# x + alpha * fx on one core: chunks of 16 rows with a tail of smaller ones, and alpha spread by a matmul

One core of one Trainium2 chip. The metric is the time of the kernel on the device in microseconds (us); lower is better. "Span" is the time from the first to the last instruction in the profile; the measured time is some 1.8 us longer. "Fast" means that a run agrees with the fastest of its kernel.

## The reference

```python
B, S, D = 512, 32, 640          # bf16
def reference(x, fx, alpha):    # alpha: one number
    return x + alpha * fx
```

The arrays are 16384 rows of 640 numbers. Each of the 128 partitions takes 128 consecutive rows, a row being 1280 bytes. 41.94 MB are read and 20.97 MB written.

## The kernel before

```python
    alpha_bf = const_pool.tile([P, 1], alpha.dtype, name="alpha_bf")
    nc.sync.dma_start(out=alpha_bf[:], in_=alpha.to_broadcast((P, 1)))
    alpha_t = const_pool.tile([P, 1], mybir.dt.float32, name="alpha_t")
    nc.vector.tensor_copy(out=alpha_t[:], in_=alpha_bf[:])

    for c in range(nchunks):                       # 16 chunks, CH = 8 rows, io_pool has bufs=4
        rs = slice(c * CH, (c + 1) * CH)
        xt = io_pool.tile([P, CH, D], x.dtype, name="xt")
        ft = io_pool.tile([P, CH, D], fx.dtype, name="ft")
        nc.sync.dma_start(out=xt[:], in_=xv[:, rs, :])
        nc.sync.dma_start(out=ft[:], in_=fxv[:, rs, :])
        nc.vector.scalar_tensor_tensor(out=xt[:], in0=ft[:], scalar=alpha_t[:, 0:1], in1=xt[:],
                                       op0=..., op1=...)   # cut: mult, then add
        nc.scalar.dma_start(out=ov[:, rs, :], in_=xt[:])
```

Loads go out on the SP queue, stores on the ACT queue. In every transfer a partition's share of a chunk is one contiguous run; I call it a *piece* (10,240 bytes here). A transfer is 128 pieces, and the packet records show 16 completion records for it (2048 pieces and 256 such records for the 16 stores), which I read as 8 pieces of each transfer on each of the 16 DMA engines.

Of the kernel before, what the change touches and what calls it, by code (L numbers as in the profile page):

```python
# [1 line left out]

# [4 lines left out]


@with_exitstack  # L10
def kernel(
    ctx: ExitStack,
    tc: tile.TileContext,
    x: bass.AP,
    fx: bass.AP,
    alpha: bass.AP,
    out: bass.AP,
):
    nc = tc.nc
    P = nc.NUM_PARTITIONS  # L20

    xf = x.flatten_outer_dims()
    fxf = fx.flatten_outer_dims()
    of = out.flatten_outer_dims()
    N, D = xf.shape
    assert N % P == 0, (N, P)
    rows_per_part = N // P

    xv = xf.rearrange("(p n) d -> p n d", p=P)
    fxv = fxf.rearrange("(p n) d -> p n d", p=P)  # L30
    ov = of.rearrange("(p n) d -> p n d", p=P)

    CH = 1
    for cand in (8, 4, 2, 1):
        if rows_per_part % cand == 0:
            CH = cand
            break
    nchunks = rows_per_part // CH

    const_pool = ctx.enter_context(tc.tile_pool(name="const", bufs=1))  # L40
    io_pool = ctx.enter_context(tc.tile_pool(name="io", bufs=4))

    alpha_bf = const_pool.tile([P, 1], alpha.dtype, name="alpha_bf")
    nc.sync.dma_start(out=alpha_bf[:], in_=alpha.to_broadcast((P, 1)))  # L44
    alpha_t = const_pool.tile([P, 1], mybir.dt.float32, name="alpha_t")
    nc.vector.tensor_copy(out=alpha_t[:], in_=alpha_bf[:])  # L46

    for c in range(nchunks):
        rs = slice(c * CH, (c + 1) * CH)
        xt = io_pool.tile([P, CH, D], x.dtype, name="xt")  # L50
        ft = io_pool.tile([P, CH, D], fx.dtype, name="ft")
        nc.sync.dma_start(out=xt[:], in_=xv[:, rs, :])  # L52
        nc.sync.dma_start(out=ft[:], in_=fxv[:, rs, :])
        nc.vector.scalar_tensor_tensor(  # L54
            out=xt[:],
            in0=ft[:],
            scalar=alpha_t[:, 0:1],
            in1=xt[:],
            op0=mybir.AluOpType.mult,
            op1=mybir.AluOpType.add,  # L60
        )
        nc.scalar.dma_start(out=ov[:, rs, :], in_=xt[:])


# [1 line left out]
_INS = ['x', 'fx', 'alpha']  # L66
_OUTS = [((512, 32, 640), 'bfloat16')]


# [23 lines left out]
```

## Time and profile before

| | before |
|---|---|
| time, median of 4 runs | 158.67 us (158.57 to 158.87) |
| span of the profiled run | 156.8 us |
| VectorE busy | 89.0 us, 57% |
| bytes moved | 62.92 MB, 401 GB/s over the span |
| no transfer at all near the end | 148.5 to 152.4 us |

The engines that move data are the bound: they are full from about 4 us to 148 (DMA share 1.01 from 4 to 16 and from 20 to 146 us). VectorE has time to spare, except behind the very last load, where nothing is left to run beside it. The prediction shows the lines.

### The profile page before, as it was taken

The page shows a single profiled execution, that of the slowest core. Times are in us where ns is not written, and L with a number is a line of the kernel's source. Part 1 is how long each engine was busy: PE and PEld are TensorE (multiplying, and loading weights), DVE is VectorE, ACT ScalarE, POOL GpSimd, SP SyncE. Part 2 cuts the span into 40 slices and gives each one's busy share as a digit, 9 for nine tenths or more (in the row PEclk, how much of TensorE's full clock was granted, in tenths as well). Part 3 has the DMA queues.
Part 4 walks back from the last instruction along what each step waited for, and adds up shares of the span by engine and source line. Part 5 has one row for each costly group of instructions (what it writes and reads, how often), then busy time and mean ns, then how long its engine had stood idle before and what let it go on. Part 6 is the DMA issues. An engine that isn't in the chain of part 4 may idle for free.

```text
span 156.8 us, 154 instructions
## 1 busy us (share of the span) xinstructions
DVE 89.0 (57%) x17; POOL 0.2 (0%) x4
## 2 busy tenths in 40 slices
DVE  0029873908558292855919285491927649193760
POOL 0000000000000000000000000000000000000000
DMA  3999999999999999999999999999999999999716
GB/s 60 410 428 426 392 400 421 428 434 434 421 428 434 431 426 423 436 428 426 431 431 426 426 434 431 423 426 426 439 423 426 426 436 426 426 423 436 316 76 259
DMA packets 7056, 62.92 MB, mean 401 GB/s; under 512 B 912, under 2 KB 912, under 8 KB 912
## 3 DMA queue, kind: packets, MB, share of 16 engines
q1 hardware_dynamic: 4752, 41.95, 64.1%
q10 hardware_dynamic: 2304, 20.97, 31.6%
HBM read 41.94 MB, written 20.97 MB: 401 GB/s over the span
## 4 chain that ended last, share of the span: by engine, by line
DMA 80%; DVE 14%; SPq 1%; issue 1%; DVEq 0%
DMA ft<-in_fx_dram 61%; DMA out_dram<-xt 19%; DVE xt L54 14%; SPq L52 1%; SPq L44 0%; DVEq L54 0%
## 5 line engine op out<-in xcount | busy, mean ns | idle before, releaser
L54 DVE SCALAR_TENSOR_TENSOR xt<-ft,alpha_t,xt 128x5120 bf16<-128x5120 bf16 x16 | 88.8, 5552 | 58.7 <-DMA ft<-in_fx_dram 58.7
L46 DVE CAST alpha_t<-alpha_bf 128x1 f32<-128x1 bf16 x1 | 0.2, 154 | 3.8 <-DMA alpha_bf<-in_alpha_dram 3.8
L77 POOL MEMSET const-bfloat16-1.0<- 128x1 bf16 x1 | 0.1, 101 | 0.0
L77 POOL MEMSET const-uint8-127<- 128x1 uint8 x1 | 0.1, 101 | 0.0
L77 POOL MEMSET const-float32-0.0<- 128x1 f32 x1 | 0.1, 98 | 0.2 <-issue 0.2
L77 POOL MEMSET const-float32-1.0<- 128x1 f32 x1 | 0.1, 98 | 0.0
## 6 DMA issues: line engine op xcount, KB each, us to landing
xt<-in_x_dram SPq DMA_DIRECT2D x16, 1280.0 KB, 17.3
ft<-in_fx_dram SPq DMA_DIRECT2D x16, 1280.0 KB, 20.4
out_dram<-xt ACTq DMA_DIRECT2D x16, 1280.0 KB, 10.2
alpha_bf<-in_alpha_dram SPq DMA_DIRECT2D x1, 0.2 KB, 3.1
```

The lines of the kernel that those rows point to most:

```text
L46: nc.vector.tensor_copy(out=alpha_t[:], in_=alpha_bf[:])
L52: nc.sync.dma_start(out=xt[:], in_=xv[:, rs, :])
L54: nc.vector.scalar_tensor_tensor(out=xt[:], in0=ft[:], scalar=alpha_t[:, 0:1], in1=xt[:], op0=mybir.AluOpType.mult, op1=mybir.AluOpType.add,)
L77: nc = _bacc.Bacc("TRN2", target_bir_lowering=False, num_devices=1)
```

## The change

It means to cut fixed costs: fewer and larger transfers in the middle (16 rows, three buffers), a tail of 8, 4 and 4 rows with buffers of their own so that less is exposed at the end, and alpha read as one element and spread to the partitions by a matmul with a row of ones, off the queue of the loads.

```diff
-    io_pool = ctx.enter_context(tc.tile_pool(name="io", bufs=4))
-    alpha_bf = const_pool.tile([P, 1], alpha.dtype, name="alpha_bf")
-    nc.sync.dma_start(out=alpha_bf[:], in_=alpha.to_broadcast((P, 1)))
+    alpha_sb = const_pool.tile([1, 1], alpha.dtype, name="alpha_sb")
+    nc.scalar.dma_start(out=alpha_sb[:], in_=alpha.rearrange("(a b) -> a b", b=1))
+    ones_row = const_pool.tile([1, P], alpha.dtype, name="ones_row")
+    nc.vector.memset(ones_row[:], 1.0)
+    alpha_ps = psum_pool.tile([P, 1], mybir.dt.float32, name="alpha_ps")
+    nc.tensor.matmul(alpha_ps[:], ones_row[:], alpha_sb[:], start=True, stop=True)
     alpha_t = const_pool.tile([P, 1], mybir.dt.float32, name="alpha_t")
-    nc.vector.tensor_copy(out=alpha_t[:], in_=alpha_bf[:])
+    nc.vector.tensor_copy(out=alpha_t[:], in_=alpha_ps[:])
 ... (cut: a function that would choose the sizes; it is overridden by the next line)
+        sizes = [16] * 7 + [8, 4, 4]
+        x_pool = ctx.enter_context(tc.tile_pool(name="xio", bufs=MAIN_BUFS))     # 3
+        f_pool = ctx.enter_context(tc.tile_pool(name="fio", bufs=MAIN_BUFS))     # 3
+        tail_pool = ctx.enter_context(tc.tile_pool(name="tail", bufs=1))
+        for ci, ch in enumerate(sizes):
+            if ch == MAX_CH:                                                     # 16
+                xt = x_pool.tile([P, MAX_CH, D], x.dtype, name="xt")
+                ft = f_pool.tile([P, MAX_CH, D], fx.dtype, name="ft")
+            else:
+                xt = tail_pool.tile([P, ch, D], x.dtype, name="xt", tag=f"xt_t{ci}")
+                ft = tail_pool.tile([P, ch, D], fx.dtype, name="ft", tag=f"ft_t{ci}")
 ... (cut: loads, compute and store as before)
```

More of the change, by code (lines that the diff above doesn't have):

```diff
@@ L7, with _chunk_schedule @@
 from concourse._compat import with_exitstack
+def _chunk_schedule(rows_per_part: int, max_ch: int) -> list[int]:
+    tail = []
+    c = max_ch // 2
+    t = 0
+    while c >= 1:
+        tail.append(c)
+        t += c
+        if c == 1:
+            tail.append(1)
+            t += 1
+            break
+        c //= 2
+    sizes = []
+    remaining = rows_per_part
+    while remaining - max_ch >= t:
+        sizes.append(max_ch)
+        remaining -= max_ch
+    while remaining > t:
+        c = min(max_ch, remaining - t)
+        sizes.append(c)
+        remaining -= c
+    for c in tail:
+        if remaining <= 0:
+            break
+        c = min(c, remaining)
+        sizes.append(c)
+        remaining -= c
+    if remaining > 0:
+        sizes.append(remaining)
+    assert sum(sizes) == rows_per_part, (sizes, rows_per_part)
+    assert all(s >= 1 for s in sizes), sizes
+    return sizes
 @with_exitstack
@@ L20 @@
     P = nc.NUM_PARTITIONS
+    dsize = mybir.dt.size(x.dtype)
     xf = x.flatten_outer_dims()
@@ L25 @@
     N, D = xf.shape
-    assert N % P == 0, (N, P)
-    rows_per_part = N // P
-    xv = xf.rearrange("(p n) d -> p n d", p=P)
-    fxv = fxf.rearrange("(p n) d -> p n d", p=P)
-    ov = of.rearrange("(p n) d -> p n d", p=P)
-    CH = 1
-    for cand in (8, 4, 2, 1):
-        if rows_per_part % cand == 0:
-            CH = cand
-            break
-    nchunks = rows_per_part // CH
-    const_pool = ctx.enter_context(tc.tile_pool(name="const", bufs=1))
-    io_pool = ctx.enter_context(tc.tile_pool(name="io", bufs=4))
@@ L43 @@
-    alpha_bf = const_pool.tile([P, 1], alpha.dtype, name="alpha_bf")
-    nc.sync.dma_start(out=alpha_bf[:], in_=alpha.to_broadcast((P, 1)))
-    alpha_t = const_pool.tile([P, 1], mybir.dt.float32, name="alpha_t")
-    nc.vector.tensor_copy(out=alpha_t[:], in_=alpha_bf[:])
-    for c in range(nchunks):
-        rs = slice(c * CH, (c + 1) * CH)
-        xt = io_pool.tile([P, CH, D], x.dtype, name="xt")
-        ft = io_pool.tile([P, CH, D], fx.dtype, name="ft")
-        nc.sync.dma_start(out=xt[:], in_=xv[:, rs, :])
-        nc.sync.dma_start(out=ft[:], in_=fxv[:, rs, :])
-        nc.vector.scalar_tensor_tensor(
-            out=xt[:],
-            in0=ft[:],
-            scalar=alpha_t[:, 0:1],
-            in1=xt[:],
-            op0=mybir.AluOpType.mult,
-            op1=mybir.AluOpType.add,
-        )
-        nc.scalar.dma_start(out=ov[:, rs, :], in_=xt[:])
+    MULT = mybir.AluOpType.mult
@@ new lines @@
+    ADD = mybir.AluOpType.add
+    const_pool = ctx.enter_context(tc.tile_pool(name="const", bufs=1))
+    psum_pool = ctx.enter_context(tc.tile_pool(name="psum", bufs=1, space=bass.MemoryType.PSUM))
+    alpha_sb = const_pool.tile([1, 1], alpha.dtype, name="alpha_sb")
[3 more added lines that the diff above has]
+    alpha_ps = psum_pool.tile([P, 1], mybir.dt.float32, name="alpha_ps")
@@ new lines, with compute @@
+    nc.tensor.matmul(alpha_ps[:], ones_row[:], alpha_sb[:], start=True, stop=True)
+    alpha_t = const_pool.tile([P, 1], mybir.dt.float32, name="alpha_t")
+    nc.vector.tensor_copy(out=alpha_t[:], in_=alpha_ps[:])
+    def compute(o_ap, f_ap, x_ap, np_=P):
+        nc.vector.scalar_tensor_tensor(
+            out=o_ap,
+            in0=f_ap,
+            scalar=alpha_t[:np_, 0:1],
+            in1=x_ap,
+            op0=MULT,
+            op1=ADD,
+        )
+    rows_per_part = N // P
+    n_main = rows_per_part * P
@@ new lines, with sbuf_need @@
+    if rows_per_part > 0:
+        xv = xf[0:n_main].rearrange("(p n) d -> p n d", p=P)
+        fxv = fxf[0:n_main].rearrange("(p n) d -> p n d", p=P)
+        ov = of[0:n_main].rearrange("(p n) d -> p n d", p=P)
+        MAIN_BUFS = 3
+        usable = (nc.sbuf_top - nc.sbuf_base) - 8 * 1024
+        def sbuf_need(ch):
+            sizes_ = _chunk_schedule(rows_per_part, ch)
+            tail_rows = sum(s for s in sizes_ if s != ch)
+            return dsize * D * (2 * MAIN_BUFS * ch + 2 * tail_rows)
+        MAX_CH = 1
+        for cand in (16, 8, 4, 2, 1):
+            if cand <= max(1, rows_per_part) and sbuf_need(cand) <= usable:
+                MAX_CH = cand
+                break
+        assert sbuf_need(MAX_CH) <= usable, ("rows too large for SBUF", D)
+        sizes = [16] * 7 + [8, 4, 4]
+        x_pool = ctx.enter_context(tc.tile_pool(name="xio", bufs=MAIN_BUFS))
+        f_pool = ctx.enter_context(tc.tile_pool(name="fio", bufs=MAIN_BUFS))
+        tail_pool = ctx.enter_context(tc.tile_pool(name="tail", bufs=1))
+        r0 = 0
+        for ci, ch in enumerate(sizes):
+            rs = slice(r0, r0 + ch)
+            r0 += ch
+            if ch == MAX_CH:
[4 more added lines that the diff above has]
+                ft = tail_pool.tile([P, ch, D], fx.dtype, name="ft", tag=f"ft_t{ci}")
+            nc.sync.dma_start(out=xt[:, :ch, :], in_=xv[:, rs, :])
+            nc.sync.dma_start(out=ft[:, :ch, :], in_=fxv[:, rs, :])
+            compute(xt[:, :ch, :], ft[:, :ch, :], xt[:, :ch, :])
+            nc.scalar.dma_start(out=ov[:, rs, :], in_=xt[:, :ch, :])
+        assert r0 == rows_per_part
@@ L66 @@
+    rem = N - n_main
+    if rem > 0:
+        rem_pool = ctx.enter_context(tc.tile_pool(name="rem", bufs=1))
+        xr = rem_pool.tile([rem, D], x.dtype, name="xr")
+        fr = rem_pool.tile([rem, D], fx.dtype, name="fr")
+        nc.sync.dma_start(out=xr[:], in_=xf[n_main:N, :])
+        nc.sync.dma_start(out=fr[:], in_=fxf[n_main:N, :])
+        compute(xr[:], fr[:], xr[:], np_=rem)
+        nc.scalar.dma_start(out=of[n_main:N, :], in_=xr[:])
 _INS = ['x', 'fx', 'alpha']
```

## The prediction

> **What bounds the kernel now.** I read the slices and the queue table first, then the groups, the chain of waits, and last the busy table by stretches. The page, part 2, 3 and 5:
>
> ```profile
> DMA  3999999999999999999999999999999999999716
> GB/s 60 410 428 426 392 400 421 428 434 434 421 428 434 431 426 423 436 428 426 431 431 426 426 434 431 423 426 426 439 423 426 426 436 426 426 423 436 316 76 259
> ...
> q1 hardware_dynamic: 4752, 41.95, 64.1%
> q10 hardware_dynamic: 2304, 20.97, 31.6%
> ...
> L54 DVE SCALAR_TENSOR_TENSOR xt<-ft,alpha_t,xt 128x5120 bf16<-128x5120 bf16 x16 | 88.8, 5552 | 58.7 <-DMA ft<-in_fx_dram 58.7
> ```
>
> The reader is to see that the sixteen DMA engines are full in every slice but the first and the last three, and that VectorE (DVE, 88.8 us in all) waits for the fx loads. So the middle is bound by moving 62.92 MB; only its two ends, and the bytes per second, can be improved. The busy table, in stretches that I chose around those ends (columns: stretch, its length, DVE busy, POOL busy, clock, DMA share, GB/s):
>
> ```profile
> 2.00:4.00 2.00, 0.15 (x1) 0.00 (x0) 1.00 0.68 128
> 4.00:16.00 12.00, 5.23 (x1) 0.00 (x0) 1.00 1.01 422
> 18.00:20.00 2.00, 2.00 (x1) 0.00 (x0) 1.00 1.02 312
> 20.00:146.00 126.00, 74.67 (x15) 0.00 (x0) 1.00 1.01 428
> ...
> 148.20:152.20 4.00, 3.32 (x1) 0.00 (x0) 1.00 0.00 0
> 152.20:155.40 3.20, 0.00 (x0) 0.00 (x0) 1.00 0.98 410
> 155.40:156.80 1.40, 0.00 (x0) 0.00 (x0) 1.00 0.01 0
> ```
>
> This is a ledger of the span. Moving everything at 428 GB/s takes 62.92 / 0.428 = 147.0 us. The rest is lost time: 2.0 us before anything moves; 1.4 us of the next 2.0 (128 instead of 428 GB/s); 0.55 us in the dip when the first store starts (312); **a hole of 4.0 us with no transfer at all**; 1.4 us from the last byte to the end of the span. Sum 156.35 of 156.8; some 0.45 us lies at the edges of my stretches. The hole in the timeline:
>
> ```profile
> 145.97 5.55 DVE L54 SCALAR_TENSOR_TENSOR xt<-ft,alpha_t,xt 128x5120 bf16<-128x5120 bf16 x1 [3.64 <-DMA ft<-in_fx_dram]
> ```
>
> and, of the chain (start us, us, what):
>
> ```profile
> 125.42 20.43 DMA ft<-in_fx_dram
> 145.85 0.03 issue
> 145.88 0.05 DVEq L54
> 145.93 0.04 issue
> 145.97 5.55 DVE xt L54
> ```
>
> The last load lands at 145.85, the previous store runs dry at 148.2, but the last chunk is in VectorE until 151.5 and its store moves bytes only from 152.2. Measured time of the profiled run less its span is 158.59 - 156.8 = 1.8 us; I add it to every span below.
>
> [...] with loads and stores of equal 10,240-byte pieces both queued, the packet records of the trace show equal numbers (from 45 to 49 us, while one store was moving, 82 pieces of loads and 83 of stores). It has no case of unequal pieces, and that is where this change goes. [...]
>
> **The change part by part.**
>
> Alpha. The broadcast of 128 two-byte pieces, at the head of the SP queue, is gone. SP spent 0.54 us on its issue before the first x load (starts 0.73 and 1.33), so x starts about 0.6 us sooner; and these small pieces no longer sit in the engines. In its place come one element by the ACT queue, a matmul with a row of ones, and a copy out of PSUM. Alpha landed 3.1 us after its issue before; even at twice that it is ready long before the first chunk of 16 rows, which lands at about 1.5 + 1.2 + 5.24/0.428 + 0.5 = 15.5 us. Not on the path. Gain 0.5 to 0.8 us.
>
> Chunks of 16 rows instead of 8. The bytes are the same; pieces per partition grow from 10,240 to 20,480 bytes. A piece costs one engine 10240 / (428/16) = 382.8 ns[...]. [...] 384 pieces per engine become 168 + 24 + 48 = 240[...]. I take 0.5.
>
> VectorE: [...]as before, never the bound.
>
> Buffers: 3 of 16 rows instead of 4 of 8. One period is 7.86 MB / 0.428 = 18.4 us, so a slot has 55 us. A store took 10.2 us from issue to landing before (3.5 of it until its first packet, behind pieces already queued; then some 6 us at half share). Doubled that is 19 to 20 us; with 11 us of VectorE 24 us are left for the next pair of loads, which need 18.4 at the shared rate. Before, it was 36.8 - 10.2 - 5.6 = 21 for 9.2. The cushion shrinks from 12 us to 6 but stays positive, and loads that are late merely leave the engines to the stores. No cost.
>
> The tail of 8, 4, 4 rows in buffers of their own. This is the part that aims at the hole. [...] How much of this shows as a hole depends on what stores are left then. I walk it from T, the landing of the last 16-row loads, with pieces of 0.76, 0.38 and 0.19 us taken in strict alternation. Store 5 (issued at T-7, begun at about T-1.5 behind queued pieces) alternates with the first half of the 8-row loads until T+7.7. Loads have the engines alone until store 6 (VectorE done T+11, first packet about T+13.5): the 8-row chunk lands, and the first 4-row chunk nearly. Then the 16 pieces of the last chunk's loads alternate with eight of store 6 (8 x 0.95 = 7.6 us, T+21) and eight of store 7 (8 x 0.57, T+25.8). So the small loads at the very end are held up by large store pieces. What is left is store 8, 1.5 us, to T+27.3; the last VectorE operation ends at about T+29.3, its store moves from T+30.2. **Hole 2.9 us instead of 4.0.**
>
> Sum: 1.5 start + 1.2 ramp + 0.55 dip + 0.45 edges + (147.0 - 0.5) + 1.4 end + 2.9 hole = 154.5 us of span, 156.3 us of time.
>
> **The rivals.** (A) *Turns are equal in bytes, or fewer pieces are queued ahead.* Then in the walk the last 1.31 MB of loads pass beside an equal amount of store 6 in 6.1 us, land at about T+20, VectorE ends at T+23.5, and stores 6 (rest), 7 and 8 keep the engines full until T+27.7: hole 0, span 151.6, time 153.4. [...] Against: the alternation that the trace shows is by pieces. (B) *Half-way:* what is queued ahead of a store is limited in bytes, not pieces (the trace can't tell, all are alike); the store of the big chunk then starts some 3 us sooner, and the hole falls to about 1: 154.4. (C) *No rate gain, and the hole stays:* larger pieces go at 428 like the small ones and the last chunk waits as in my walk or a little longer (hole 3.5): 157.4. (D) *Three buffers are too few:* the load queue runs dry more than once. Each gap needs both queues empty, and the chunks' stores follow each other closely, so I give it little; it would cost 1 to 3 us and land at 157 to 159.
>
> **Range and chances.** My walk 156.3, weight 0.5; rival A 153.4, 0.2; B 154.4, 0.15; C and D 157.4 and up, 0.15. The middle of that is near 155.7, the range 153.2 to 157.5. Faster by over 2% means under 155.5 us: all of A and B and a part of the walk's own spread: 0.44. Slower by 2% needs 161.8 us, more than losing the whole gain: 0.01.
>
> **What would show it.** The middle stretch at 428 to 432 GB/s: over 430 means a cost per piece. First packets at about 1.5 us. The table over the last 15 us: a stretch of zero DMA of about 3 us, and the last two fx loads landing late (with 4-row chunks some 6 us apart or more) speak for alternation by pieces; no such stretch, and VectorE done well before the last big store, for A. Zero-DMA stretches between 40 and 120 us would be D. I am wrong altogether if the time is over 158.7 (the bound was not transfer) or under 152[...].

The sum came to 154.5 us of span and 156.3 us of time. The 0.5 us taken for larger pieces was an estimate of mine (a_pieces_half gives 0.6). The hole of 2.9 us contains about 2.9 us of VectorE for the last 4-row chunk, in the step from T+25.8 to T+29.3 (half of the measured 5.55 us would be 2.8; the changed kernel's trace has 2.88). The same path in the kernel before, from the last load's last byte to the last store's first, took 7.0 us in the packet records (145.43 to 152.40): 0.4 until the load landed, 0.1, 5.55 of VectorE, and 0.9 from VectorE's end to the first piece. That pieces of unequal size alternate too was an assumption here; a_f_eighth shows it (103 packets to 96).

## The result, and the profile after

The changed kernel took **152.81 us** (median of 8 runs, 152.64 to 153.11) against 158.70 us for the kernel before (12 runs of the same rounds). The ratio is 0.9633, 95% interval 0.9624 to 0.9643. Ratios here are the mean time of one kernel's fast runs over that of the other's of the same rounds, so they are not quite the ratio of the medians that I quote. The gain is 3.7%, or 5.8 us. My 155.7 was too high, and the result lies 0.4 us under my range.

The page of the changed kernel, parts 2 and 3 (slices; queues with packets, MB and share; q1 are the loads, q10 the stores), and of its groups by shape the three of the main VectorE operation. The packets of a view are pieces and, for each transfer, 16 completion records of 4 bytes: the 2880 of q1 are 2560 pieces and 320 such records.

```profile
DMA  5999999999999999999999999999999999999995
GB/s 173 433 433 433 433 433 433 363 417 433 433 433 428 433 433 433 428 433 433 433 428 433 428 433 433 433 433 428 433 417 422 433 422 409 424 417 456 406 422 217
...
q1 hardware_dynamic: 2880, 41.94, 65.8%
q10 hardware_dynamic: 1442, 20.97, 32.4%
```

```profile
L80 DVE SCALAR_TENSOR_TENSOR xt<-ft,alpha_t,xt 128x10240 bf16<-128x10240 bf16 x7 | 76.2, 10884 | 55.7 <-DMA ft<-in_fx_dram 55.7
L80 DVE SCALAR_TENSOR_TENSOR xt<-ft,alpha_t,xt 128x2560 bf16<-128x2560 bf16 x2 | 5.7, 2876 | 0.0
L80 DVE SCALAR_TENSOR_TENSOR xt<-ft,alpha_t,xt 128x5120 bf16<-128x5120 bf16 x1 | 5.5, 5544 | 0.0
```

The empty slices at the end are gone: the engines are full from the second slice to the last but one. VectorE takes 10.88, 5.54 and 2.88 us for chunks of 16, 8 and 4 rows. The busy table of the changed kernel (stretch, length, PE, PEld, DVE, POOL busy, clock, DMA share, GB/s):

```profile
0.00:1.70 1.70, 0.00 (x0) 0.10 (x1) 0.17 (x1) 0.20 (x4) 1.00 0.00 0
1.70:4.00 2.30, 0.16 (x1) 0.00 (x0) 0.16 (x1) 0.00 (x0) 1.00 1.05 338
4.00:26.00 22.00, 0.00 (x0) 0.00 (x0) 10.62 (x1) 0.00 (x0) 1.00 1.01 433
26.00:36.00 10.00, 0.00 (x0) 0.00 (x0) 8.71 (x2) 0.00 (x0) 1.00 0.99 387
36.00:122.00 86.00, 0.00 (x0) 0.00 (x0) 45.97 (x5) 0.00 (x0) 1.00 1.01 433
...
137.80:143.00 5.20, 0.00 (x0) 0.00 (x0) 5.20 (x3) 0.00 (x0) 1.00 1.02 437
143.00:146.30 3.30, 0.00 (x0) 0.00 (x0) 2.26 (x1) 0.00 (x0) 1.00 0.95 403
146.30:150.00 3.70, 0.00 (x0) 0.00 (x0) 0.00 (x0) 0.00 (x0) 1.00 0.85 354
150.00:151.20 1.20, 0.00 (x0) 0.00 (x0) 0.00 (x0) 0.00 (x0) 1.00 0.00 0
```

Two things are to be seen. In the long middle the view has 433 GB/s where it had 428. It counts a piece wholly where it starts; spread over their durations, the packet records make it 431.5 GB/s from 36 to 122 us, against 428.7 over the same stretch of the kernel before. And after the last load (its last piece ends at 137.8) there is work for the engines without a pause until 150.0, while VectorE ends at 145.3 (2.26 us into the stretch that starts at 143.00). The first and last data piece in the packet records close the ledger of both kernels:

| us | before | after | gain |
|---|---|---|---|
| span start to first load piece | 2.53 | 1.72 | 0.81 |
| moving 62.92 MB, hole left out | 149.21 | 148.28 | 0.93 |
| hole (no transfer) | 3.92 | 0 | 3.92 |
| last piece to end of span | 1.15 | 1.27 | -0.12 |
| span | 156.81 | 151.27 | 5.54 |

So 71% of the gain in span (3.92 of 5.54) is the hole at the end. I had let three quarters of it stand.

### The profile page after: what moved, and what is told of

The parts are those of the page before. It is cut to its first block, busy times and chain, and to the rows that moved or that the text cites. A ratio compares the mean times of both kernels' runs of the same rounds, so it can differ in the third digit from the quotient of the medians.

```text
span 151.3 us, 118 instructions
## 1 busy us (share of the span) xinstructions
PE 0.2 (0%) x1; PEld 0.1 (0%) x1; DVE 87.6 (58%) x12; POOL 0.2 (0%) x4
## 2 busy tenths in 40 slices
DMA packets 4322, 62.92 MB, mean 416 GB/s; under 512 B 482, under 2 KB 482, under 8 KB 1250
## 3 DMA queue, kind: packets, MB, share of 16 engines
q1 hardware_dynamic: 2880, 41.94, 65.8%
## 4 chain that ended last, share of the span: by engine, by line
DMA 79%; DVE 12%; DVEq 2%; SPq 2%; issue 1%
DMA xt<-in_x_dram 37%; DMA ft<-in_fx_dram 31%; DVE xt L80 12%; DMA out_dram<-xt 11%; DVEq L166 2%; SPq L126 1%; SPq L127 1%; DVEq L80 0%
## 5 line engine op out<-in xcount | busy, mean ns | idle before, releaser
L80 DVE SCALAR_TENSOR_TENSOR xt<-ft,alpha_t,xt 128x10240 bf16<-128x10240 bf16 (+2 forms) x10 | 87.2, 8748 | 55.7 <-DMA ft<-in_fx_dram 55.7
```

The source lines that it names most:

```text
L80: nc.vector.scalar_tensor_tensor(out=o_ap, in0=f_ap, scalar=alpha_t[:np_, 0:1], in1=x_ap, op0=MULT, op1=ADD,)
```

## The experiments

Each was timed beside the kernel before on the same chip, and every one gave the right result. They answer three questions: which part of the change is worth what, how the two queues share an engine, and why the hole went away altogether. After reading the changed kernel's trace I had a new theory: in it, 10,240-byte load pieces passed two for one beside 20,480-byte store pieces (71 to 40 from 122.6 to 126.4 us in the packet records), which looks like turns equal in *bytes*, not pieces. If so, my walk was wrong in its rule. That theory fell.

| run | what differs | time, us | ratio to before (95% interval) |
|---|---|---|---|
| changed kernel | | 152.81 | 0.9633 (0.9624 to 0.9643) |
| b_alpha | before + alpha part | 157.46 | 0.9925 (0.9914 to 0.9937) |
| b_taper | before + last 8 rows as 4, 4 | 155.09 | 0.9774 (0.9761 to 0.9786) |
| b_alpha_taper | before + both | 153.73 | 0.9688 (0.9675 to 0.9701) |
| a_alpha_sp | changed, alpha as before | 154.00 | 0.9711 (0.9698 to 0.9723) |
| a_alpha_act | changed, broadcast on ACT | 153.62 | 0.9679 (0.9666 to 0.9693) |
| a_notaper | changed, eight chunks of 16 | 159.58 | 1.0046 (1.0028 to 1.0064) |
| a_tail88 | changed, tail 8, 8 | 152.89 | 0.9635 (0.9622 to 0.9648) |
| a_pieces_half | changed, pieces of 10,240 bytes | 153.41 | 0.9674 (0.9661 to 0.9687) |
| a_pieces_quarter | changed, pieces of 5,120 bytes | 154.91 | 0.9764 (0.9751 to 0.9777) |
| a_f_quarter | changed, fx pieces of 5,120 bytes | 153.97 | 0.9710 (0.9697 to 0.9723) |
| a_f_eighth | changed, fx pieces of 2,560 bytes | 155.53 | one run, state unknown |
| c_20rows | chunks of 20, tail 12, 8, 8 | 155.90 | 0.9822 (0.9808 to 0.9835) |

Differences in us below are differences of ratios times 158.7; the intervals make such a difference uncertain by some 0.2 to 0.3 us.

**b_alpha: the alpha part alone.**

```diff
 (kernel before)
-    nc.sync.dma_start(out=alpha_bf[:], in_=alpha.to_broadcast((P, 1)))
+    (the lines of the changed kernel: one element on ACT, ones, matmul, copy)
```

> The kernel before with only the new way of alpha (one element on the ACT queue, a matmul with ones, a copy out of PSUM). My theory, that the ledger's start term is due to this part: the first load piece moves 0.8 us sooner (1.7 instead of 2.5 us), nothing else changes, the hole of 3.9 us stays: 157.9 us. Rival, that an earlier start is lost again because the middle is set by buffers coming free: 158.7 us.

Measured 157.46 us, a gain of 1.2 us. The first load piece starts at 1.72 instead of 2.53 us, as expected, and the hole stays (147.21 to 151.16 in the packet records). The 0.4 us more than expected come in the first transfer, which then takes 4.03 instead of 4.39 us.

**b_taper: the small tail alone.**

```diff
 (kernel before)
-    for c in range(nchunks):
+    for c, ch in enumerate([8] * 15 + [4, 4]):     # the two of 4 in buffers of their own
```

> The kernel before with only its last chunk of 8 rows cut into two of 4 with buffers of their own. Theory (turns of loads and stores equal in bytes, the tail is what fills the hole): the hole falls from 3.9 us to under 1 us, time 155.0 to 155.4 us. Rival (turns by pieces, small loads held up by large store pieces): a hole of 1.5 to 2 us is left, 156.3 us. Rival (the chunk of 16 rows carries the gain): 158 us.

Measured 155.09 us, a gain of 3.6 us, and no hole is left. The number is the one expected of turns in bytes, but the reason given is wrong: while the first 4-row loads (5,120-byte pieces) ran beside a store of 10,240-byte pieces, from 137 to 141 us, the queues' packets were nearly one for one and the bytes were not (packets, MB, share; the 112 are 96 pieces and 16 completion records, so it is 119 to 112 with the records counted and 119 to 96 without):

```profile
q10 hardware_dynamic: 119, 1.22, 71.6%
q1 hardware_dynamic: 112, 0.49, 29.6%
```

No stretch without transfers follows the last load (the busy table, columns stretch, length, DVE, POOL, clock, DMA share, GB/s):

```profile
145.80:150.00 4.20, 3.14 (x2) 0.00 (x0) 1.00 0.94 396
150.00:152.00 2.00, 0.00 (x0) 0.00 (x0) 1.00 0.84 341
```

The loads were indeed slowed, but only those of the first 4-row chunk (3.6 and 3.1 us from first to last piece, against 1.8 and 2.1 for the second); the last load piece ended at 145.80, hardly later than in the kernel before (145.43), and what VectorE has to do after it is 2.9 instead of 5.6 us.

**a_alpha_sp: alpha as before, all else changed.**

```diff
 (changed kernel)
-    (one element on ACT, ones, matmul, copy out of PSUM)
+    nc.sync.dma_start(out=alpha_bf[:], in_=alpha.to_broadcast((P, 1)))
```

> The changed kernel with the broadcast of alpha at the head of the SP queue put back. Theory: it starts 0.8 us later and ends 0.8 us later, 153.6 us. Rival: the alpha part is worth nothing, 152.8 us.

Measured 154.00 us, a loss of 1.2 us. The part is worth the same in both kernels, so an earlier start goes through to the end, as it must where the engines never rest.

**a_notaper: 16-row chunks to the end.**

```diff
 (changed kernel)
-        sizes = [16] * 7 + [8, 4, 4]
+        sizes = [16] * 8
```

> The changed kernel with eight chunks of 16 rows and no tail. Theory: the last chunk lands at about 138.3 us, VectorE has it until 149.2, the store before ends at 143.8, so a hole of 6.3 us opens, and the last store of 2.62 MB runs to 156.2; span 157.5, time 159.2 us, slower than the kernel before. Rival (larger chunks and pieces carry the gain): under 155 us.

Measured 159.58 us, slower than the kernel before, as expected, if only by 0.5%. The six runs lie in two groups, two at 158.8 and 158.9 us and four at 159.6 to 159.8; the profile is of one of the two. The busy table has the hole where it was to be, its length set by VectorE's 10.88 us on the last chunk:

```profile
137.40:143.40 6.00, 0.00 (x0) 0.00 (x0) 5.49 (x1) 0.00 (x0) 1.00 0.89 382
143.50:149.60 6.10, 0.00 (x0) 0.00 (x0) 5.30 (x1) 0.00 (x0) 1.00 0.00 0
```

So the larger chunks without the tail lose, although the alpha part is in this run too; the tail is what makes them usable. It is worth 6.5 us here.

**a_pieces_half and a_pieces_quarter: the same transfers in smaller pieces.** Gaps of 32 bytes in the tiles break each partition's run, so that counts of transfers, waits and chunks stay.

```diff
 (changed kernel; k = 2, for quarters k = 4; the DRAM side is viewed in the same shape)
-                xt = x_pool.tile([P, MAX_CH, D], x.dtype, name="xt")
+                xt = x_pool.tile([P, 2, 8 * D + 16], x.dtype, name="xt")
+                xt = xt[:, :, : 8 * D]
 (and ft likewise)
```

> The changed kernel with a gap of 32 bytes in the middle of each 16-row row of the x and fx tiles, so that the same transfers, with the same counts, waits and chunks, are made of 10,240-byte pieces instead of 20,480. 168 pieces per engine become 336. Theory (a cost per piece): by the durations of single pieces in the trace (761 ns against 2 x 385) 9 ns each, 1.5 us in all, 154.3 us; by the throughput of the two kernels, after the alpha part is taken off, nearer 4 ns each, 153.5 us. Rival (piece size costs nothing at these sizes): 152.8 us.

> The same with three gaps, pieces of 5,120 bytes, 504 more pieces per engine than the changed kernel. Theory: three times the loss of the halved pieces: 154.8 us at 4 ns a piece, 157.3 us at 9 ns. Rival: 152.8 us.

Measured 153.41 and 154.91 us, 0.65 and 2.1 us more than the changed kernel. For 168 and 504 more pieces on each engine that is 3.9 and 4.1 ns a piece: a cost per piece, in proportion, at the lower of the two values that I had put down (the intervals allow 2.3 to 5.4 and 3.6 to 4.6 ns). The change itself saves 144 pieces an engine, so 0.6 us.

These two runs also settle how long a store waits behind loads. In the stretch from the end of VectorE's work on the fifth chunk to just before the first piece of its store, no store piece moves. What the load queue moved in it (packets, MB, share of the engines), in the changed kernel from 97.75 to 101.2 us:

```profile
q1 hardware_dynamic: 84, 1.39, 94.0%
```

in the halved pieces from 97.75 to 101.1:

```profile
q1 hardware_dynamic: 151, 1.42, 100.4%
```

and in the quartered from 98.7 to 102.1:

```profile
q1 hardware_dynamic: 288, 1.42, 101.2%
```

Of these packets 16, 12 and 11 are completion records; the pieces are 68, 139 and 277, as 1 to 2.0 to 4.1, and the bytes are the same. The packet records give 3.4 to 3.6 us from VectorE's end on this chunk to the first piece of its store in all three, and 3.4 to 3.5 for most stores of the kernel before (the first two wait about 4, and the last, with the engines idle, 0.9). **What stands ahead of a store is an amount of bytes or time, not a number of pieces.**

**a_f_quarter and a_f_eighth: how the two queues take turns.**

```diff
 (changed kernel, k = 4; for the eighth k = 8; xt stays in one piece)
-                ft = f_pool.tile([P, MAX_CH, D], fx.dtype, name="ft")
+                ft = f_pool.tile([P, 4, 4 * D + 16], fx.dtype, name="ft")
+                ft = ft[:, :, : 4 * D]
```

> The changed kernel with gaps only in the fx tiles: fx loads in pieces of 5,120 bytes, x loads and stores in 20,480. It tells how an engine shares itself between the two queues. Turns equal in bytes: while a store and an fx load both move, four load pieces pass for one store piece, a 16-row store still takes about 12 us, and the time is that of the halved pieces or so (168 more pieces). Turns by pieces (what my walk assumed): one for one, the load gets a fifth of the bytes, and a store beside an fx load takes under 9 us.

> The same with fx pieces of 2,560 bytes. Turns equal in bytes: eight load pieces for one store piece, a store still takes 12 us. Turns by pieces: one for one, under 8 us for a store beside an fx load.

Turns in bytes are refuted. With 2,560-byte fx pieces beside a store of 20,480-byte pieces (44 to 49.5 us, where only these two move):

```profile
q10 hardware_dynamic: 103, 2.11, 89.1%
q1 hardware_dynamic: 96, 0.25, 11.1%
```

One for one in packets, eight to one in bytes. With 5,120-byte pieces, from 44 to 50 us, it is 103 packets of the store (2.01 MB; 5 are completion records) to 112 of the loads (0.57 MB). The second store took 8.2 and 7.0 us in the two kernels by the packet records, against 12.0 in the changed one. So the rule of my walk was right. The packet records show it engine by engine: linked where one ends and the next starts, the store's pieces mostly stand between single load pieces or completion records, here and in the changed kernel, where the view has 97 packets of each queue from 103 to 112 us. My two-for-one reading of the changed kernel came from a stretch, up to 126.4 us, in which most engines were already done with that store (13 of 16 by 125.8 us), each having only eight pieces of it; a short stretch summed over 16 engines can't show a rule of one engine. The times, 153.97 and (one run) 155.53 us, are 1.2 us and some 2.7 us over the changed kernel, for 168 and 392 more pieces: about 7 ns a piece, more than the 4 above. What the rest is I did not find out.

**a_alpha_act: the broadcast on the other queue.**

```diff
 (changed kernel)
-    (one element on ACT, ones, matmul, copy out of PSUM)
+    nc.scalar.dma_start(out=alpha_bf[:], in_=alpha.to_broadcast((P, 1)))
```

> The changed kernel with the broadcast of alpha (128 two-byte pieces) kept, but issued on the ACT queue, and no matmul. It parts the 1.2 us that the alpha part was worth in both kernels. Theory: 0.8 us are the SP issue ahead of the first load, 0.4 us the 128 small pieces that delay the first large ones, so 153.2 us. Rival (only the place in the SP queue counts): 152.8 us. Rival (only the pieces count): 154.0 us.

Measured 153.62 us, 0.7 us over the changed kernel: the two shares come out the other way round. Leaving the SP queue is worth 0.5 us, not issuing 128 small pieces 0.7, each to about 0.3, so which is the larger is near the noise. The transfer itself shows turns by pieces once more: 0.2 KB needed 12.5 us from issue to landing (in the kernel before, ahead of the loads on their own queue, 3.1). Its first piece moves 4.6 us after the issue; the eight on each engine then mostly stand one by one between 20,480-byte load pieces of 0.76 us, and the last ends 6.8 us later:

```profile
alpha_bf<-in_alpha_dram ACTq DMA_DIRECT2D x1, 0.2 KB, 12.5
```

**a_tail88: a coarser tail.**

```diff
 (changed kernel)
-        sizes = [16] * 7 + [8, 4, 4]
+        sizes = [16] * 7 + [8, 8]
```

> The changed kernel with a tail of 8 and 8 rows instead of 8, 4, 4. Theory (after the last 16-row chunk VectorE works without a pause until about 145.3 us, and the stores of that chunk and of the first 8 rows keep the engines full until about 147): no hole, 152.7 to 153.0 us, as good as 8, 4, 4. Rival (the last chunk has to be small, as the 5.5 us of VectorE behind the last load are exposed): 1.5 to 3 us slower, 154.3 us or more.

Measured 152.89 us, the same as 8, 4, 4 within the intervals. VectorE ends at 144.4 us, the store before the last one keeps the engines until 146.4, and there is no hole (stretch, length, PE, PEld, DVE, POOL, clock, DMA share, GB/s):

```profile
143.00:146.00 3.00, 0.00 (x0) 0.00 (x0) 1.42 (x1) 0.00 (x0) 1.00 0.99 420
146.00:149.50 3.50, 0.00 (x0) 0.00 (x0) 0.00 (x0) 0.00 (x0) 1.00 0.89 377
```

The last chunk need not be as small as 4 rows; it needs enough store traffic still to move while VectorE works on it.

**b_alpha_taper: both small parts, chunks of 8.**

> The kernel before with the alpha part and with the last 8 rows cut into 4 and 4, chunks of 8 rows and four buffers kept. If the parts add up (1.2 us and 3.6 us): 153.9 us, and 1.1 us are left for chunks and pieces of 16 rows, of which the halved pieces explain 0.6. If they overlap: 154.4 us or more.

Its edit is those of b_alpha and b_taper together. Measured 153.73 us, a gain of 4.9 to 5.0 us where the two parts alone make 1.2 + 3.6 = 4.8: they add up. From here to the changed kernel it is 0.9 us, of which the pieces explain 0.6; the other 0.3 is near the width of the intervals, and I leave it open.

**c_20rows: an attempt to beat both.**

```diff
 (changed kernel)
-        sizes = [16] * 7 + [8, 4, 4]
+        MAX_CH = 20
+        sizes = [20] * 5 + [12, 8, 8]
-        f_pool = ctx.enter_context(tc.tile_pool(name="fio", bufs=MAIN_BUFS))
+        f_pool = ctx.enter_context(tc.tile_pool(name="fio", bufs=2))
 (the chunk of 12 uses a main buffer, the two of 8 their own)
```

> An attempt to beat both: chunks of 20 rows (pieces of 25,600 bytes), fx in two buffers, tail of 12, 8, 8. 192 pieces per engine instead of 240, at 4 ns each 0.2 us, and three transfers fewer at the end: 152.5 us if the theory of the tail holds. If two fx buffers hold loads back or the large chunks open a hole: over 153.5 us.

It failed, at 155.90 us, and it failed in the way that I had foretold for the changed kernel. A 20-row store was in flight when the tail's loads came, then a 12-row store. From 136 to 141 us 10,240-byte load pieces alternate with 15,360-byte store pieces (queues, then the busy table):

```profile
q10 hardware_dynamic: 90, 1.32, 61.7%
q1 hardware_dynamic: 84, 0.86, 40.4%
```

```profile
136.00:142.60 6.60, 0.00 (x0) 0.00 (x0) 0.00 (x0) 0.00 (x0) 1.00 1.02 436
142.60:146.20 3.60, 0.00 (x0) 0.00 (x0) 2.45 (x1) 0.00 (x0) 1.00 0.88 373
146.30:150.10 3.80, 0.00 (x0) 0.00 (x0) 3.00 (x1) 0.00 (x0) 1.00 0.00 0
```

VectorE idles from 136 to 142.6 with the engines full, as the last load, issued at 108.2 us, dribbles in until 142.6. Then VectorE works with nothing left to move beside it: a hole of 3.8 us. The run changes chunks, tail and buffers at once, so it shows that the hole comes about in this way, not which of the three sets it off. I know of no version that beats the changed kernel; a_tail88 equals it.

## Why the prediction was wrong

*What bounds it, and the ledger.* Right. The transfers are the bound, only the ends and the cost per byte can gain, and the terms of the ledger can be read off again after the change.

*Alpha.* Right in direction, too small: 0.5 to 0.8 us put down, plus 0.2 of ramp in the sum, 1.2 measured in both kernels. The small pieces cost more than I gave them (0.7 us, a_alpha_act).

*Pieces.* Right: I took 0.5 us, an estimate; 144 pieces fewer at 4 ns (a_pieces_half) are 0.6. The middle runs at 431.5 GB/s by the packet records (433 in the view), against 428.7 before.

*VectorE, three buffers.* Right: 87.2 us of these operations (88.8 before), and no pause of the engines in the middle.

*The tail.* This is the step that failed: "Hole 2.9 us instead of 4.0". It is 0, and 2.9 of the 3.2 us by which the span was over-estimated are this term (154.5 put down, 151.3 measured). The rule of turns was not at fault: pieces do alternate one for one (a_f_eighth, b_taper, c_20rows). The clock of the walk was. (One count in the prediction was misread: from 45 to 49 us the view has 86 store pieces, not 83, to 82 of loads.) I write it out from VectorE's start on the last 16-row chunk, 123.3 us in the trace, as T:

| | put down | measured |
|---|---|---|
| store 5 issued | T-7 | T-11.2 |
| its first piece | T-1.5 | T-7.7 |
| its last piece ends | T+7.7 | T+3.3 |
| store 6, first piece | T+13.5 | T+13.8 |
| last load piece ends | T+25.8 | T+14.5 |
| VectorE ends | T+29.3 | T+21.9 |
| store 8, last piece ends | T+27.3 | T+24.7 |

Two assumptions made the difference. I took a steady period of 18.4 us; with three buffers the chunks come in a limp instead, VectorE starting at 15.4, 27.5, 50.2, 64.9, 86.8, 101.2 and 123.3 us, that is 12 to 15 and 22 us apart in turn (their mean is what I had). So store 5 was issued 11 us, not 7, ahead of T. And I took the queue ahead of a store as seven or eight pieces, which with double pieces is 5 to 6 us; it is the same 1.4 MB as before, and the wait stayed 3.5 us. The timeline of the changed kernel has the first part (start, us, engine, line, operation):

```profile
101.19 10.88 DVE L80 SCALAR_TENSOR_TENSOR xt<-ft,alpha_t,xt 128x10240 bf16<-128x10240 bf16 x1 [3.50 <-DMA ft<-in_fx_dram]
...
123.32 21.94 DVE L80 SCALAR_TENSOR_TENSOR xt<-ft,alpha_t,xt 128x10240 bf16<-128x10240 bf16 x4 [11.24 <-DMA ft<-in_fx_dram]
134.24 11.39 ACTq L129 DMA_DIRECT2D out_dram<-xt  x4
```

With both, store 5 was out of the way at T+3.3, the loads had the engines alone for 10.5 us instead of 5.8, and all of them were through when store 6 began. The queues from 126.6 to 137.1 us:

```profile
q1 hardware_dynamic: 760, 4.39, 100.5%
q10 hardware_dynamic: 1, 0.00, 0.0%
```

From T on, VectorE then never waited again: its last four operations stand in the timeline as one block of 21.94 us. Stores 6, 7 and 8 covered it. An estimate parts the two: the same walk, redone strictly piece by piece for one engine with 0.76, 0.38 and 0.19 us a piece (the medians in the packet records are 0.761, 0.385 and 0.196), leaves a hole of 3.8 us as put down, some 2.5 with the wait alone mended, some 1 with the time of issue alone, and none with both. By this estimate the even period is the larger error. That the two made the hole is worked out, not shown one by one; shown are the lag that stays (the pieces runs), the limp and the free run of the loads (the trace), and that with loads caught beside large store pieces the foretold hole does open (c_20rows). The margin is thin: the last load piece ended 0.6 us after store 6's first one. Why the chunks limp, and why the queue ahead of a store holds 1.4 MB, I did not test.

*The rivals.* B (the queue ahead limited in bytes) was the true half of it, and I gave it 0.15; its hole of about 1 us still carried the even period. A (no hole, 153.4 us) was near in time; its first reading, turns equal in bytes, is false, and its second, fewer pieces queued ahead, is what B says too. The sign that I had put down for A, no stretch without transfers, came true although its rule is false: that sign doesn't part the rules, as it also depends on when the stores start. D did not happen. The chance of 0.44 for a gain over 2% leaned the wrong way.

## What to carry to other kernels

These are the lessons of one kernel. Where transfers bound a streaming kernel, write the span as first byte + bytes / rate + holes + end, and look for the holes at the ends: cutting the last chunk of 8 rows in two, alone, gave 3.6 of the 5.8 us. Give the last large chunk enough small loads behind it to cover its compute, and the last small chunk enough stores; larger chunks without such a tail lost time (a_notaper, 159.58 us against 158.7). Keep small pieces, loads or constants, from running beside large pieces of another queue, as they got one turn for one here (103 packets with 2.11 MB to 96 with 0.25 MB in a_f_eighth); and when you walk through a tail by hand, take the start times from the trace's own rhythm and not from an even period.
